# Two more head pairs in cluster order, sorted beside the first batch: routing attention and PReLU feed-forward

## The chip, the cores and the metric

The kernel runs on one core of a Trainium2 chip, as one launch. The metric is the device time of that launch in microseconds (us); less is better. Times given as "the runs" are timed executions without a profiler; the profile is one further execution, recorded by the hardware profiler.

## The reference

Attention with a mask by clusters, then a feed-forward network with PReLU, all in float32 (the weights come as float64):

```
q, k, v: (4 batches, 8 heads, 768 tokens, 64)      centroids: (8 heads, 16, 64)
q_assign = argmax(normalised q . normalised centroids);  k_assign likewise
mask     = q_assign[:, None] == k_assign[None, :]         # same cluster
attn     = softmax(where(mask, q k^T / 8, -1e9));  x = attn v  -> (3072 tokens, 512)
h = x @ w_in (512 x 2048);  g = max(h, 0) + alpha * min(h, 0);  out = g @ w_out (2048 x 512)
```

A query sees only the keys of its own cluster, so most of the 768 x 768 scores of a head are masked away.

## The kernel before, in words

Two heads make a pair; pairs are numbered n = 0 to 15, four to a batch. The work on one pair is cut into steps. An unordered pair has two halves of 384 queries, and each half has three steps; in it all 768 keys meet those queries, key chunk by key chunk of 128: scores on PE (`score`, L784), exponential on ACT (L802, L805), the mask on DVE (L825; pairs 0 to 3 have it added on PE at L793), sums of the exponentials (`add_up` L835 on DVE, or on PE at L932 in steps 0 to 12), weighing of v on PE (`weigh`, L939). Then the row sums are inverted and spread (L907 to L914, or L945 to L955 in the first steps) and `normalise` (L1042) writes the result to a tile xT. A pair in cluster order takes three steps for both halves. Its tokens were sorted by cluster in advance, so that a chunk of keys meets only a window of queries near it (`window`, 224, 320 or 384 columns in place of twice 384), and `weigh_near` (L972) does likewise; the result is then turned to rows (`to_rows`, L1002), scattered back to token order (`put_back`, L1011, indirect DMA from POOL), fetched and transposed (`fetch_back`, `turn_back`, L1030).

The sort of a pair (`order_features`, `order_sims`, `order_counts`, `order_begins`, `order_ranks`, `order_rows`, `order_clusters`) is some 20 DVE operations spread over slots. Then `order_stage` (L661, SP) loads rows of q, k and v, 24 calls of `order_scatter` (L675, POOL) write them to a scratch in DRAM in cluster order, and `order_load` (L681 on, SP) reads them back. Ahead of each group of scatters `pace` puts a small copy on ACT (L651) and one on POOL that waits for it (L652); eight such tokens may be open.

The weights are converted from float64 in 32 tiles (`convert`): SP loads a tile to one of the raw buffers (L247), `split` is two DVE operations (L253, L255), `scale` two on ACT (L259, L261), `join` two on DVE (L265, L268) and a multiply on POOL (L271). Conversions are begun by `convert_next` at fixed slots; `advance` puts scale 4 slots after split and join 2 after that.

Order is written out by hand. A loop over steps u (0 to 23 are batch 0, with the conversion; from 24 on the rest) with five slots to a step emits everything; each engine works in that order. `later(k, piece)` emits a piece k slots on, `prep_at` and `load_at` hold what is due at a step. The FFN of each finished half (`ffn_pieces`: `hidden` L1066 with L1072 and L1058, `final` L1084) is cut into pieces that are fed between the steps' slots: FFN of batch 0, half 0, in steps 12 to 23, then one half at a time. The last batch's FFN (L1246, L1302) comes at the end with nothing beside it. In the kernel before, pairs from NO = 9 on are in cluster order: batch 2 begins with 9, 10 and 11, then 8; batch 3 is 12 to 15.

Of the kernel before, what the change touches and what calls it, by code (L numbers as in the profile page):

```python
# [19 lines left out]
P = 128  # L20
# [3 lines left out]
def kernel(  # L24
# [49 lines left out]
    ps_m = fast.enter_context(tc.tile_pool(name="ps_m", bufs=1, space=PS))  # L74
    ps_f = fast.enter_context(tc.tile_pool(name="ps_f", bufs=2, space=PS))
    fast.enter_context(tc.manual_schedule())
    first_part = fast.enter_context(ExitStack())
    memp = first_part.enter_context(tc.tile_pool(name="memp", bufs=NCH))
    raws = first_part.enter_context(tc.tile_pool(name="raws", bufs=1))
    cvt = first_part.enter_context(tc.tile_pool(name="cvt", bufs=3))  # L80

    early = []

# [18 lines left out]


    pairs = [(b, hp) for b in range(B) for hp in range(NCH)]
    NO = WHOLE * NCH - 3
    NP = len(pairs)
    raw_qk, vts = {}, {}

# [130 lines left out]

    CW = 512  # L240

    raw_tiles = [raws.tile([P, CW, 2], U32, name=f"raw{i}") for i in range(5)]

    def convert(src, dst):
        raw = raw_tiles[0]
# [51 lines left out]
    def advance(stages):  # L297
        stages.pop(0)()
        if stages:
            later(4 if len(stages) == 2 else 2, lambda: stages and advance(stages))  # L300
        elif stages is under_way[0]:
            under_way.popleft()
            converted[0] += 1
# [184 lines left out]
    assert NX * TS == S and 2 * TS == P  # L488
    PARTS = 3
    STAGES = 2  # L490
    us, ranks, orders, scratch, sorts = {}, {}, {}, {}, {}
    sorting = deque()

    def second_part():

        first_part.close()
        for name, bufs in (("emore", 1), ("ordc", 1), ("ordp", 1), ("order", NP - NO),
                           ("xmore", 1), ("byrow", 1), ("pace", 8)):
            sorts[name] = fast.enter_context(tc.tile_pool(name=name, bufs=bufs))
        for i in range(5):  # L500
            e_tiles.insert(0, sorts["emore"].tile([P, 2, HS], FP32, name=f"more{i}"))

    def order_constants():
# [54 lines left out]
                                    scalar2=None, op0=ALU.add)  # L558
        for i, piece in enumerate((columns, sums_before, sums_within, shifts)):
            later(5 + i, piece)  # L560
        begins = ordc.tile([P, NP - NO], FP32, name="begins")
        sorts.update(stage=stage, number=number, place=place, before=before, within=within,
                     shift=shift, begins=begins)

# [40 lines left out]
    def order_ranks(n, ps):  # L605
        member, count = us.pop(n)
        ordp, order = sorts["ordp"], sorts["order"]
        begin = ordp.tile([P, 2], FP32, name="begin")
        nc.vector.tensor_tensor(out=begin, in0=ps[:, 0:2], in1=sorts["shift"], op=ALU.add)
        nc.vector.tensor_copy(out=sorts["begins"][:, n - NO:n - NO + 1], in_=ps[:, 0:1])  # L610
        nc.vector.scalar_tensor_tensor(out=count, in0=count, scalar=begin[:, 1:2],
                                       in1=member, op0=ALU.add, op1=ALU.mult)
        later(1, lambda: order_rows(n, begin, count))
# [113 lines left out]
    assert NJ == GROUP * SB and SB == GT  # L727
    steps, begun_at, feeds = [], [], {}
    for b in range(B):
        whole = [n for n in range(b * NCH, (b + 1) * NCH) if n >= NO]  # L730
        rest = [n for n in range(b * NCH, (b + 1) * NCH) if n < NO]
        begun_at.append(len(steps))
        steps += [(n, None, s) for n in whole for s in range(SB)]
        for half in range(2) if rest else ():
            if half and not whole:
                begun_at.append(len(steps))
            steps += [(n, half, s) for n in rest for s in range(SB)]
            feeds[len(steps)] = [(b, 0), (b, 1)] if whole else [(b, half)]
    begun_at.append(len(steps))
    assert NJ == 6 and GROUP == 2  # L740

# [133 lines left out]
        accTs[n, half] = accT  # L875

    def rows_sums(n, half):
        near = n >= NO
        if not near or half == 0:
            parts[n] = rdp.tile([P, 1 + near, 2, NX], FP32, name="parts" if near else "part")  # L880
        nc.vector.tensor_reduce(
            out=parts[n][:, half if near else 0].rearrange("p h x -> p (h x)"),
            in_=accTs.pop((n, half)), axis=AX.X, op=ALU.add)
# [25 lines left out]
            spread_out(n, half, inv)  # L909

    def spread_out(n, half, inv):
        pool = sorts["ordp"] if n >= NO and half else rdp
        rd = rds[n, half] = pool.tile([P, HS], FP32, name="rd")
        nc.vector.transpose(out=rd, in_=inv[:, :, None].broadcast_to((P, NX, Q)))  # L914

# [117 lines left out]

    def x_tile(b, half):
        if (b, half) not in xTs:
            pool = sorts["xmore"] if (b, half) == (WHOLE - 1, 1) else xpool
            xTs[b, half] = pool.tile([P, NCH, HS], FP32, name="xT")
        return xTs[b, half]

# [102 lines left out]
    def last_pieces():  # L1142
# [195 lines left out]
            return [p1, p5, p6, p2, p7, p3, p4]  # L1338

        def room_for_y():  # L1340
            t = sorts["xmore"].tile([P, NCH, HS], FP32, name="xT").rearrange(
                "p c q -> p (c q)")
# [22 lines left out]
    FREE = SLOTS * SB - 3  # L1365


    ORDERS = [26, 29, 35, 38, 41, 56, 60]
    LEADS = [4, 3, 4, 4, 3, 3, 3]
    prep_at, load_at = {}, {}  # L1370
    for (n, half), u in start_of.items():
        def at(step, slot, piece):
            prep_at.setdefault((step, slot), []).append(piece)
        if half is None:
            t = ORDERS[n - NO]
# [4 lines left out]
            load_at.setdefault(u - LEADS[n - NO], []).append(  # L1380
                lambda n=n: order_load(n))
            at(u - 4, 0, lambda n=n: prep_clusters(n))
            for i in range(2):
                at(u - 1, i, lambda n=n, i=i: order_blocks(n, i))
                at(u - 1, FIRST + i, lambda n=n, i=i: order_queries(n, i))
            continue
        if half == 0:
            if n < NCH:
                if n > 1:
                    load_at.setdefault(max(u - 7, 0), []).append(lambda n=n: load(n))  # L1390
                if n > 0:
                    load_at.setdefault(max(u - 6, 0), []).append(lambda n=n: load_v(n))
            else:
                load_at.setdefault(u - (9 if u < 2 * TOGETHER else 10), []).append(
                    lambda n=n: load(n))
# [8 lines left out]
            at(u - (3 if n < NCH else 5 if u - 6 < TOGETHER else 6), FIRST,  # L1404
               lambda n=n: prep_sims(n)) if u - 6 < 2 * TOGETHER else at(
                   u - 6, FIRST + 1, lambda n=n: prep_sims(n))
# [14 lines left out]
    def scatters_at(v, s, i):  # L1421


        if v < SB:
            return 1 + (s == 0 or i == 0)
        if v < 3 * SB:
            return 0
        if v < 4 * SB:
            return int(s == 0 or i == 0)
        return 1 + (s == 0 or i % 2 == 0)  # L1430

    def feed(pieces):
        for _ in range(pieces):
# [27 lines left out]
    for u in range(-AHEAD, TOGETHER):  # L1461
        for piece in load_at.get(u, []):
            piece()
        n, half, s = steps[max(u, 0)]
        prior = steps[max(u - 1, 0)]
        ended = u > 0 and prior[2] == SB - 1
        tick()
# [26 lines left out]
            whole = len(ffn) - KEEP  # L1494
        take = (max(len(ffn) - KEEP - whole * (UB - 1 - u % UB) // UB, 0) if ffn else 0)

        converting = 0 if u < 0 else (2, 0, 2, 2, 0, 2, 1, 1, 1, 1, 1, 1)[u] if u < UB else 2
        for i in range(SLOTS - FIRST):
            tick()
            feed(take * (i + 1) // 3 - take * i // 3)  # L1500
# [4 lines left out]
                convert_next()  # L1505
            if u >= -1:
                fetch(3 if u < UB else 2)
        if s == SB - 1 and u >= UB:
            total(n)
    assert not sources and not under_way and not unfinished[0]  # L1510
# [5 lines left out]
    for u in range(TOGETHER, NS + 1):  # L1516
# [49 lines left out]
            slots = range(3, SLOTS)  # L1566
        else:
            slots = range(SLOTS)
        if u == TOGETHER + 1:
            order_constants()  # L1570
        for i in slots:
            tick()
            if s == 0:
# [39 lines left out]
    NN, m = NP - NO, 2 * NC  # L1613
# [204 lines left out]
```

## Time and profile before

| | us |
|---|---|
| median of 3 runs | 952.11 |
| the runs | 950.09, 952.11, 956.48 |
| the profiled execution, whole | 932.13 |
| its span | 930.4 |
| PE busy in the span | 916.0 |
| DVE busy | 654.3 |
| POOL busy | 389.1 |
| ACT busy | 262.2 |

The granted clock of TensorE is 1.00 over the whole span. Matmuls overlap in the records, so the busy time of a group of matmuls counts an overlapped stretch once, while the mean of one does not; a matmul of float32 stands as two records. Busy PE is not PE at its peak. The scores of step 6 begin at 46.0 us, those of step 12 at 73.3, those of step 24 at 195.4, those of step 48 (the first pair in cluster order) at 439.2.

### The profile page before, as it was taken

The page shows a single profiled execution, that of the slowest core. Times are in us where ns is not written, and L with a number is a line of the kernel's source. Part 1 is how long each engine was busy: PE and PEld are TensorE (multiplying, and loading weights), DVE is VectorE, ACT ScalarE, POOL GpSimd, SP SyncE. Part 2 cuts the span into 40 slices and gives each one's busy share as a digit, 9 for nine tenths or more (in the row PEclk, how much of TensorE's full clock was granted, in tenths as well). Part 3 has the DMA queues.
Part 4 walks back from the last instruction along what each step waited for, and adds up shares of the span by engine and source line. Part 5 has one row for each costly group of instructions (what it writes and reads, how often), then busy time and mean ns, then how long its engine had stood idle before and what let it go on. Part 6 is the DMA issues. An engine that isn't in the chain of part 4 may idle for free.

```text
span 930.4 us, 11983 instructions
## 1 busy us (share of the span) xinstructions
PE 916.0 (98%) x3963; PEld 494.6 (53%) x3963; DVE 654.3 (70%) x1246; ACT 262.2 (28%) x660; POOL 389.1 (42%) x579
## 2 busy tenths in 40 slices
PE   8999999999999999999999999999999999999997
PEld 5534444445445454455555554555555555556886
DVE  5797788889769699598997899764647135598200
ACT  5764454223123122232222332122222121221000
POOL 2433232200006768587766787677723470000000
PEclk9999999999999999999999999999999999999999
DMA  8433659028001625453762283643511012000000
GB/s 301 132 123 93 148 128 159 18 56 179 26 1 51 153 73 145 88 107 85 156 133 42 50 136 96 142 87 95 97 37 27 12 38 54 1 0 1 23 23 26
DMA packets 226708, 77.71 MB, mean 84 GB/s; under 512 B 210752, under 2 KB 214544, under 8 KB 226640
## 3 DMA queue, kind: packets, MB, share of 16 engines
q1 hardware_dynamic: 217728, 62.72, 30.6%
q0 software_dynamic: 8064, 13.78, 4.7%
q8 instruction: 33, 0.54, 0.3%
q10 hardware_dynamic: 848, 0.39, 0.2%
q14 instruction: 35, 0.29, 0.1%
HBM read 52.25 MB, written 24.25 MB: 82 GB/s over the span
## 4 chain that ended last, share of the span: by engine, by line
PE 94%; DVE 4%; issue 1%; POOL 0%; ACT 0%; DVEq 0%; ACTq 0%; POOLq 0%
PE fps L1066 27%; PE fps L1084 27%; PE sps L784 7%; PE vps L939 7%; PE sps L1302 4%; PE sps L1246 4%; PE fps L784 3%; PE vps L1246 2%; PE vps L1302 2%; PE vps L972 1%; PE mps L972 1%; PE fps L1302 1%; PE fps L1246 1%; PE sps L793 1%; PE mps L894 1%
## 5 line engine op out<-in xcount | busy, mean ns | idle before, releaser
L1066 PE MATMUL fps<-xT,w_in_sb 128*128 128x384 f32 x768 | 259.3, 491 | 0.0
L1084 PE MATMUL fps<-w_out_sb,gT 128*128 128x512 f32 x576 | 254.1, 595 | 0.3 <-DVE gT L1058 0.3
L675 POOL DMA_INDIRECT scratch<-stage,off x168 | 181.3, 1079 | 67.1 <-DMA stage<-in_v_dram 29.5
L1066 PEld LDWEIGHTS fps<-xT,w_in_sb 128*128 128x128 f32 x768 | 142.3, 190 | 103.2 <-issue 4.9
L1084 PEld LDWEIGHTS fps<-w_out_sb,gT 128*128 128x128 f32 x576 | 107.5, 190 | 132.2 <-issue 122.6
L1072 ACT COPY gT<-fps 128x384 f32<-128x384 f32 x96 | 46.0, 479 | 235.9 <-PE fps L1066 235.9
L652 POOL COPY paced<-pace 1x1 f32<-1x1 f32 x204 | 55.0, 270 | 135.7 <-ACT pace L651 135.2
L1058 DVE SCALAR_TENSOR_TENSOR gT<-gT,alpha 128x384 f32<-128x384 f32 x96 | 61.5, 648 | 60.8 <-ACT gT L1072 60.7
L1011 POOL DMA_INDIRECT back<-rows,off x84 | 85.6, 1018 | 22.2 <-issue 16.5
L784 PE MATMUL sps<-qkT 64*128 64x384 f32 (+1 forms) x464 | 85.0, 485 | 0.0
L805 ACT ACTIVATE E<-sps 128x768 f32<-128x768 f32 (+1 forms) x76 | 56.3, 786 | 62.1 <-PE sps L793 39.7
L784 PEld LDWEIGHTS sps<-qkT 64*128 64x128 f32 x464 | 41.2, 186 | 38.6 <-issue 15.5
L825 DVE SCALAR_TENSOR_TENSOR more<-aq,key,more 128x384 f32<-128x384 bf16 (+2 forms) x116 | 60.4, 579 | 0.0
L939 PE MATMUL vps<-E,vt 128*64 128x384 f32 x292 | 54.2, 495 | 1.5 <-DVE xT L1042 1.5
L271 POOL TENSOR_TENSOR w_in_sb<-w_in_sb,power 128x512 f32<-128x512 f32 x16 | 26.9, 1684 | 67.4 <-DVE w_in_sb L268 67.4
L271 POOL TENSOR_TENSOR w_out_sb<-w_out_sb,power 128x512 f32<-128x512 f32 x16 | 22.5, 1411 | 56.0 <-DVE w_out_sb L268 56.0
L825 DVE SCALAR_TENSOR_TENSOR E<-aq,key,E 128x384 f32<-128x384 bf16 (+2 forms) x88 | 45.0, 569 | 0.6 <-ACT E L802 0.6
L835 DVE TENSOR_TENSOR acc<-acc,E 128x768 f32<-128x768 f32 x35 | 33.3, 951 | 14.5 <-ACT E L805 13.6
L907 DVE RECIPROCAL inverses<-mps 64x12 f32<-64x12 f32 (+1 forms) x42 | 10.5, 249 | 45.7 <-PE mps L894 39.8
L1090 ACT COPY y<-fps 128x512 f32<-128x512 f32 x18 | 10.6, 587 | 99.2 <-PE fps L1084 99.2
L1092 DVE TENSOR_TENSOR y<-y,fps 128x512 f32<-128x512 f32 x24 | 16.4, 682 | 27.6 <-PE fps L1084 27.6
L805 ACT ACTIVATE more<-sps 128x768 f32<-128x768 f32 (+1 forms) x40 | 29.2, 764 | 12.2 <-PE sps L784 11.8
(284 smaller groups left out, 1174.1 us busy)
## 6 DMA issues: line engine op xcount, KB each, us to landing
raw<-in_moe_w_in_dram SPq DMA_DIRECT2D x16, 512.0 KB, 5.2
raw<-in_moe_w_out_dram SPq DMA_DIRECT2D x16, 512.0 KB, 4.3
out_dram<-y SPq DMA_DIRECT2D x21, 256.0 KB, 2.4
qk<-scratch SPq DMA_DIRECT2D x56, 96.0 KB, 3.5
qk<-in_q_dram SPq DMA_DIRECT2D x48, 96.0 KB, 3.6
qk<-in_k_dram SPq DMA_DIRECT2D x48, 96.0 KB, 3.6
w_in_kept<-w_in_sb SPq DMA_DIRECT2D x8, 512.0 KB, 3.3
vt<-in_v_dram SPq DMA_DIRECT2D x9, 384.0 KB, 6.5
```

Source lines behind the costliest of these rows:

```text
L652: nc.gpsimd.tensor_copy(out=sorts["paced"], in_=token)
L675: nc.gpsimd.indirect_dma_start(out=scratch[n][1][h * NX + xx], out_offset=bass.IndirectOffsetOnAxis(ap=ranks[n][:, xx, h:h + 1], axis=0), ...
L784: nc.tensor.matmul(out=bank(ps, h, m), lhsT=qkT[r:r + D, S + c * P:S + (c + 1) * P], rhs=qkT[r:r + D, tokens], start=True, stop=not early_ ...
L805: nc.scalar.activation(out=E[:, :, 0:m], in_=ps[:, :, 0:m], func=AF.Exp, scale=SCALE)
L825: nc.vector.scalar_tensor_tensor(out=e, in0=of, scalar=keys[n][:, NJ + c, h:h + 1], in1=e, op0=ALU.is_equal, op1=ALU.mult)
L939: nc.tensor.matmul(out=po[r:r + D, 0:HS], lhsT=vts[n][:, h, c, :], rhs=e[:, h, :], start=(c == 0), stop=(c == NJ - 1))
L1011: nc.gpsimd.indirect_dma_start(out=to[i], out_offset=bass.IndirectOffsetOnAxis(ap=place[:, h, j:j + 1], axis=0), in_=rows[j // HJ][:, j % ...
L1058: nc.vector.scalar_tensor_tensor(out=gs[f], in0=gs[f], scalar=alpha[:, f:f + 1], in1=gs[f], op0=ALU.mult, op1=ALU.max)
L1066: nc.tensor.matmul(out=ps[:, 0:HS], lhsT=w_in_sb[:, c, f * P:(f + 1) * P], rhs=xTs[b, half][:, c, :], start=(c == 0), stop=(c == NCH - 1))
L1084: nc.tensor.matmul(out=ps[:, 0:DM], lhsT=gs[f][:, i * P:(i + 1) * P], rhs=w_out_sb[:, f, :], start=on and f == f0, stop=off and f == f0 + ...
L1246: nc.tensor.matmul(out=bank[to], lhsT=w_in_form(m, x, cc), rhs=rhs[:, cc, :], start=start and cc == 0, stop=cc == KH - 1, skip_group_check ...
L1302: nc.tensor.matmul(out=bank[to], lhsT=g_form(m, x, t), rhs=w_out_form(n, x), start=start and x == 0, stop=x == NQ - 1, skip_group_check=no ...
```

## The change

Pairs 6 and 7, the last two of batch 1, are put in cluster order too. Batch 1 now begins with 6 and 7 (three steps each), then half 0 of pairs 4 and 5, then half 1; it has 18 steps in place of 24. Their sort is done in steps 7 to 23, beside batch 0 and the conversion of the weights, at the slots of the first loop. For the room that the sort's tiles take, the raw buffers go from five to three, the buffers for `power` from three to two, and the conversion's stages follow each other sooner (3 slots and 1 in place of 4 and 2). Sorts of later pairs get other steps (`ORDERS`, `LEADS`), and the scatters per slot are set anew. The core of the diff; renamed pools, index changes of the same kind and the check's wider tables are left out:

```diff
+    sorts = {name: fast.enter_context(tc.tile_pool(name=name, bufs=bufs)) for name, bufs in
+             (("ordc", 1), ("ordp", 1), ("order", 7), ("pace", 8))}
...
-    cvt = first_part.enter_context(tc.tile_pool(name="cvt", bufs=3))
+    cvt = first_part.enter_context(tc.tile_pool(name="cvt", bufs=2))
...
-    NO = WHOLE * NCH - 3
+    ORDERED = [2 * NCH - 2, 2 * NCH - 1] + list(range(WHOLE * NCH - 3, B * NCH))
+    NO = ORDERED[2]
...
-    raw_tiles = [raws.tile([P, CW, 2], U32, name=f"raw{i}") for i in range(5)]
+    raw_tiles = [raws.tile([P, CW, 2], U32, name=f"raw{i}") for i in range(3)]
...
-            later(4 if len(stages) == 2 else 2, lambda: stages and advance(stages))
+            later(3 if len(stages) == 2 else 1, lambda: stages and advance(stages))
...
-        whole = [n for n in range(b * NCH, (b + 1) * NCH) if n >= NO]
-        rest = [n for n in range(b * NCH, (b + 1) * NCH) if n < NO]
+        whole = [n for n in range(b * NCH, (b + 1) * NCH) if n in ORDERED]
+        rest = [n for n in range(b * NCH, (b + 1) * NCH) if n not in ORDERED]
...
-            feeds[len(steps)] = [(b, 0), (b, 1)] if whole else [(b, half)]
+            feeds[len(steps)] = [(b, half)] if b < WHOLE - 1 else [(b, 0), (b, 1)]
...
-        pool = sorts["ordp"] if n >= NO and half else rdp
+        pool = sorts["ordx"] if n in ORDERED and half else rdp
...
-            pool = sorts["xmore"] if (b, half) == (WHOLE - 1, 1) else xpool
+            pool = sorts["xmore"] if (b, half) in ((1, 1), (B - 1, 0)) else xpool
...
-    ORDERS = [26, 29, 35, 38, 41, 56, 60]
-    LEADS = [4, 3, 4, 4, 3, 3, 3]
+    ORDERS = [8, 11, 26, 29, 32, 35, 38, 50, 54]
+    LEADS = [4, 3, 4, 3, 4, 4, 3, 3, 3]
...
-            return 1 + (s == 0 or i == 0)
+            return 1 + (s == 0 or i != 1)
...
-        return 1 + (s == 0 or i % 2 == 0)
+        return 1 + (s == 0 or i != 1)
...
+        if u == ORDERS[0] - 1:
+            order_constants()
...
-        converting = 0 if u < 0 else (2, 0, 2, 2, 0, 2, 1, 1, 1, 1, 1, 1)[u] if u < UB else 2
+        converting = 0 if u < 0 else (2, 0, 2, 1, 1, 1, 2, 1, 1, 1, 1, 1)[u] if u < UB else 2
...
+            if sorting:
+                pace()
+            room = 1 + (i < 2)
+            while sorting and room:
+                scatters, piece = sorting.popleft()
+                piece()
+                room -= scatters
...
-        if u == TOGETHER + 1:
-            order_constants()
```

The last added block stands in the first loop's slots: with sorts pending, each of a step's last three slots takes a pace token and two, two and one scatters.

More of the change, by code (lines that the diff above doesn't have):

```diff
@@ L490 @@
     STAGES = 2
-    us, ranks, orders, scratch, sorts = {}, {}, {}, {}, {}
+    us, ranks, orders, scratch = {}, {}, {}, {}
     sorting = deque()
@@ L496, in second_part @@
         first_part.close()
-        for name, bufs in (("emore", 1), ("ordc", 1), ("ordp", 1), ("order", NP - NO),
-                           ("xmore", 1), ("byrow", 1), ("pace", 8)):
-            sorts[name] = fast.enter_context(tc.tile_pool(name=name, bufs=bufs))
+        for name in ("emore", "ordx", "xmore", "byrow"):
+            sorts[name] = fast.enter_context(tc.tile_pool(name=name, bufs=1))
         for i in range(5):
@@ L560, in order_constants @@
             later(5 + i, piece)
-        begins = ordc.tile([P, NP - NO], FP32, name="begins")
+        begins = ordc.tile([P, len(ORDERED)], FP32, name="begins")
         sorts.update(stage=stage, number=number, place=place, before=before, within=within,
@@ L609, in order_ranks @@
         nc.vector.tensor_tensor(out=begin, in0=ps[:, 0:2], in1=sorts["shift"], op=ALU.add)
-        nc.vector.tensor_copy(out=sorts["begins"][:, n - NO:n - NO + 1], in_=ps[:, 0:1])
+        i = ORDERED.index(n)
+        nc.vector.tensor_copy(out=sorts["begins"][:, i:i + 1], in_=ps[:, 0:1])
         nc.vector.scalar_tensor_tensor(out=count, in0=count, scalar=begin[:, 1:2],
@@ L734 @@
         for half in range(2) if rest else ():
-            if half and not whole:
+            if half and b < WHOLE - 1:
                 begun_at.append(len(steps))
             steps += [(n, half, s) for n in rest for s in range(SB)]
-            feeds[len(steps)] = [(b, 0), (b, 1)] if whole else [(b, half)]
+            feeds[len(steps)] = [(b, half)] if b < WHOLE - 1 else [(b, 0), (b, 1)]
     begun_at.append(len(steps))
@@ L877, in rows_sums @@
     def rows_sums(n, half):
-        near = n >= NO
+        near = n in ORDERED
         if not near or half == 0:
@@ L1340, in room_for_y @@
         def room_for_y():
-            t = sorts["xmore"].tile([P, NCH, HS], FP32, name="xT").rearrange(
+            t = xpool.tile([P, NCH, HS], FP32, name="xT").rearrange(
                 "p c q -> p (c q)")
@@ L1374 @@
         if half is None:
-            t = ORDERS[n - NO]
+            t = ORDERS[ORDERED.index(n)]
             load_at.setdefault(t, []).append(lambda n=n: load(n))
@@ L1379 @@
             at(t + 2, 2, lambda n=n: order_sims(n))
-            load_at.setdefault(u - LEADS[n - NO], []).append(
+            load_at.setdefault(u - LEADS[ORDERED.index(n)], []).append(
                 lambda n=n: order_load(n))
-            at(u - 4, 0, lambda n=n: prep_clusters(n))
+            sooner = u - 1 < TOGETHER
+            at(u - 4, FIRST if u - 4 < TOGETHER else 0, lambda n=n: prep_clusters(n))
             for i in range(2):
-                at(u - 1, i, lambda n=n, i=i: order_blocks(n, i))
-                at(u - 1, FIRST + i, lambda n=n, i=i: order_queries(n, i))
+                at(u - 1, i + FIRST * sooner, lambda n=n, i=i: order_blocks(n, i))
+                at(u - 1, FIRST + i + sooner, lambda n=n, i=i: order_queries(n, i))
             continue
@@ L1393 @@
             else:
-                load_at.setdefault(u - (9 if u < 2 * TOGETHER else 10), []).append(
+                load_at.setdefault(u - (9 if u < start_of[NO, None] else 10), []).append(
                     lambda n=n: load(n))
@@ L1404 @@
             at(u - (3 if n < NCH else 5 if u - 6 < TOGETHER else 6), FIRST,
-               lambda n=n: prep_sims(n)) if u - 6 < 2 * TOGETHER else at(
+               lambda n=n: prep_sims(n)) if u < start_of[NO, None] else at(
                    u - 6, FIRST + 1, lambda n=n: prep_sims(n))
@@ L1611 @@
                             scalar2=good[:, 1:2], op0=ALU.is_le, op1=ALU.mult)
-    NN, m = NP - NO, 2 * NC
+    NN, m = len(ORDERED), 2 * NC
     spans = const.tile([m, 4, NN], FP32, name="spans")
```

## The prediction

> **What bounds the kernel now.** I read the page's busy shares first, then the chain that ended last, then busy time by stretch, then the timelines of PE and DVE around the one place where the chain leaves PE.
>
> ```profile
> PE 916.0 (98%) x3963; PEld 494.6 (53%) x3963; DVE 654.3 (70%) x1246; ACT 262.2 (28%) x660; POOL 389.1 (42%) x579
> PE 94%; DVE 4%; issue 1%; POOL 0%; ACT 0%; DVEq 0%; ACTq 0%; POOLq 0%
> ```
>
> PE carries 94% of the chain, so a matmul saved is time saved, unless another engine is late there. The second line also says where that happens: DVE has 4%. Busy time by stretch (columns: stretch, length, then PE, PEld, DVE, ACT, POOL) shows it is local:
>
> ```profile
> 14.00:34.00 20.00, 19.24 (x188) 9.10 (x186) 13.70 (x32) 15.14 (x24) 4.17 (x2) 1.00 0.56 199
> 46.00:77.00 31.00, 29.54 (x263) 12.08 (x260) 28.42 (x59) 20.86 (x32) 12.90 (x9) 1.00 0.42 133
> 77.00:106.00 29.00, 28.75 (x104) 13.30 (x100) 20.62 (x37) 11.67 (x21) 6.37 (x4) 1.00 0.26 76
> 106.00:146.00 40.00, 40.00 (x155) 18.83 (x154) 33.06 (x60) 17.98 (x30) 11.12 (x8) 1.00 0.77 161
> ```
>
> From 46 to 77 us (steps 6 to 11 and the head of 12: half 0 of batch 0, beside the weights' conversion) DVE is busy 92%, as full as PE. The timelines of PE and DVE at that place:
>
> ```profile
> 67.66 1.51 PE L939 MATMUL vps<-E,vt 128*64 128x384 f32 x8 [1.46 <-DVE xT L1042]
> 59.09 1.50 DVE L255 TENSOR_SCALAR w_in_sb<-raw 128x512 uint32<-128x512 uint32 x1
> 72.54 1.49 DVE L253 TENSOR_SCALAR power<-raw 128x512 uint32<-128x512 uint32 x1 [1.17 <-POOL w_in_sb L271]
> ```
>
> PE stood 1.46 us for a normalisation that DVE reached late. DVE itself waited 1.17 us for a POOL multiply, then ran at a third of its speed. Last, the chain's pieces for one pair's weighing, unordered (one half) and ordered (both halves):
>
> ```profile
> 541.93 4.02 PE vps L939 x24
> ...
> 615.50 1.72 PE vps L972 x16
> 617.21 1.57 PE mps L972 x16
> ```
>
> **What the Trainium skill says.** TensorEngine Tiling (Array Packing), section When to Use Tiling: a contraction of 64 rows can be packed twice. The trace agrees: four score matmuls of 384 columns on 64 rows (8 records) take 1.49 us in the chain, four FFN matmuls on 128 rows (8 records) 2.58. So I price scores and weighing from the chain, not from the 500 ns means. SBUF — State Buffer, section Who interferes with whom: the port pair shared by VectorE and GpSimd is an exclusive lock for a whole instruction. The trace agrees: the split's second operation is 0.42 us mostly and 1.50 when POOL multiplies. TensorE: Matmul & The Clock Gate, section Architectural detail: ACT and DVE are strict FIFO. The 1.46 us above is that: the normalisation stood behind conversions in DVE's queue. Perfetto Trace Analysis, section Optimization Strategy, says that the most-contended engine can change from regime to regime; the stretches show it.
>
> **The change, part by part.**
>
> *Pairs 6 and 7 scored in windows.* Unordered, each half costs scores 4.42 us (two calls of 2.21 on the PE timeline) and weighing 4.02, so a pair 16.9. Ordered: scores 2 x 1.83, weighing 1.72 + 1.57 = 3.29, plus three transposes to rows twice (6 x 0.164 from the group's 6.9 us by 42 = 1.0) and the begin sums (0.35): 8.3. Assignment matmuls are four either way. Two pairs: 2 x 8.6 = 17.2 us off PE, from batch 1 on, where PE is busy all the time. This is the gain.
>
> *Sorting moved into steps 7 to 23.* Constants now go out at step 7, pair 6's sort at steps 8 to 13, pair 7's at 11 to 16. DVE work by the rows (us): constants 0.55 + 0.63 + 0.99 + 0.44 = 2.6; per pair, transposes of q and k 2 x 0.964 = 1.93, the six argmax operations 0.58 + 0.55 + 0.57 + 0.36 + 0.55 + 0.54 = 3.14, member 0.55, scan 0.95, ranks 0.92, offsets 1.35, clusters 1.45.
>
> *First stage, to step 12.* Before pair 3's normalisation at step 12 DVE gains constants, pair 6's transposes, argmax and member: 2.6 + 1.93 + 3.14 + 0.58 = 8.2 us. The conversions from the end of normalisation 0 (34.1) to the end of normalisation 3 (78.96) are as many as before: ten splits, eleven joins. In that stretch DVE idled only 1.16 + 1.17 + 0.53 = 2.9 us. And its queue is less well filled: the join follows its split after 3 + 1 slots in place of 4 + 2, and with one conversion a step there is often nothing between the two on DVE. Then it waits for ACT's 0.72 + 0.62 = 1.34 us. I count this for the splits of steps 4, 5 and 8 in full and for two more in part: 5 us. The scale now also stands on ACT ahead of the exponentials of the very next step (before: of the step after that), and those free the two PSUM score buffers, so DVE's lag reaches PE a step of 4.15 us earlier. The sum is 8.2 + 5 - 2.9 = 10.3. The first FFN matmul (step 12) needs all four chunks of xT, so all DVE lag must be paid there. Least: idle time swallows its 2.9 and no serial waits come, 5.3. Most: contention and POOL's constants standing before its multiplies add 3, so 13. I take 9.5.
>
> *Steps 12 to 23.* DVE gains 11 us in steps 12 to 16 (scan, pair 7's sort) and loses 7 in 17 to 20 (prep of pairs 4 and 5, now at 23 to 28). Step 13 alone asks 14.8 us of DVE against 10.5 of PE. The slopes of step 13 stood at 94.15 us, just before the last matmul that uses them, and DVE had 3.8 us of idle ahead of step 13's sums. With some 3 us more before the sums and 3.4 us of ranks, offsets and simT after them the slopes are about 3.2 late; a second, smaller stop at step 17. POOL gets five scatters a step (1.08 + 0.2 each), three pace copies and two multiplies (2 x 1.55): about 10.4 us against steps of 8.7 to 12.2, and with two power buffers the second split of a step waits for the multiply just issued, about 1 us. The raw tile for that split is loaded after a join of the same step, with 4 to 6 us of DVE work between and 4.3 to 5.2 us to land; SP takes it behind stage loads that wait for scatters. I take 4 us for all; least 2, most 10 if POOL's lag is carried over by every split.
>
> *Batches 1 and 2.* The loads of sorts 6 and 7 (12 DMAs, SP some 6 us each) go out a step or more before use. In steps 30 to 35 put-backs of 6 and 7 meet the scatters of 9 and 10: POOL is asked for 39 + 40 us against 26 + 36 of PE, so it falls about 17 us behind; the eight pace tokens then hold ACT (before, the wait of pace on POOL was 10.7 us in all, without PE stopping). DVE is 7 us behind in the first of these blocks; before, the block at 383 to 408 us was 7 behind and lost 1.7. I take 2, from 0 to 5. Then batch 1's FFN, spread over 6 steps in place of 12, makes blocks of 45 to 52 us of PE in which all catch up. SBUF-only moves (ordx, xmore, memory of the pools) and nine columns in place of seven at the end cost nothing: the last FFN covers them (PE is back to back from 851 us), or some 0.1 us uncovered.
>
> **Sum.** -17.2 + 9.5 + 4 + 2 = -1.7 us on the profiled execution of 932.1 (span 930.4), so 930.4. The runs' median, 952.1, lies 20 above that execution and their spread is 6.4; the difference is carried over: 950.4. About 1% (9.5 us) is what a measurement of this kernel tells from no change.
>
> **Rivals.**
> 1. Forecast: the saving is made on PE and mostly paid back at steps 7 to 17: 950.4, own range 944 to 958. Chance 0.50.
> 2. The front hides it: DVE's idle and the slack at 77 to 106 (20.6 of 29 busy) swallow most. Losses 5.3 + 2 + 0 = 7.3: 952.1 - 9.9 = 942; with the whole gain 935. For: over steps 0 to 23 DVE is not full on average (81% from 77 to 195). Against: the order in the queue, and 92% from 46 to 77. Chance 0.29.
> 3. Slower: POOL becomes the pacer of steps 13 to 20. Each step's multiplies stand behind five scatters, the second split waits for them, and every later DVE operation with it. At 10.4 us of POOL plus some 2 us of waits for stage loads against a mean step of 10.1, each of 8 steps loses 2 us, 16 in place of 4, with 10.3 at the front and 3 in batch 1: -17.2 + 29.3 = +12, 964. It decides once POOL needs over about 11.5 us a step. For: before, scatters waited 29.5 us for stage loads. Against: DVE may lag half a step before PE feels it. Chance 0.21.
>
> **How the numbers follow.** Faster by over 1% needs losses under 7.7 us: rival 2, 0.29. Slower by over 1%: rival 3, 0.21. The range reaches from 938, inside rival 2, to 963, close to rival 3, and leaves about 2 in 10 out.
>
> **What would show it.** Right: a first FFN matmul some 10 us later than 77.4, with PE waits for DVE xT or ACT E between 50 and 90 us; step 24's scores near 209 us in place of 195.4; DVE near 97% from 46 us on; 17 us less PE time from there to the end. Wrong: the first FFN matmul within 5 us of 77.4 (rival 2), or POOL without idle from step 13 to 20 and steps of 12 us (rival 3). If the weighing of pairs 6 and 7 were not 3.3 us each, the gain itself would be wrong.

## The result and the profile after

The changed kernel takes 983.53 us (median of four runs, 980.32 to 985.84), the kernel before 953.26 (950.09 to 956.48) beside it: a ratio of 1.0315, 95% interval 1.0268 to 1.0362. The forecast of 950.4 and its range up to 963 were both wrong; the nearest case was rival 3 (964).

The runs come from several chips, on some of which the kernel before takes 952 to 958 us (the slower kind below) and on others 933 (the faster kind), as in the profile shown of it, so the ratio of every experiment is taken against before on its own chip, and spans are compared across the two kinds only up to step 24, where the two runs of after in the table below differ by 2.4 us.

The page of after, busy shares, granted PE clock in 40 slices, and the chain that ended last:

```profile
PE 925.7 (94%) x3899; PEld 498.1 (51%) x3899; DVE 653.4 (66%) x1244; ACT 258.5 (26%) x674; POOL 468.4 (48%) x689
PEclk9978999989999989999999999899999999999999
PE 72%; DVE 12%; issue 5%; POOL 4%; DMA 3%; SPq 2%; ACT 1%; DVEq 0%; POOLq 0%; ACTq 0%
```

There are 64 matmul records fewer (3,899 against 3,963), as intended, and yet PE is busy 9.7 us longer than in before's profile, and still 2.6 us longer (918.6) in e9, a run of this kernel on a chip of before's kind: it runs part of the time at a lower clock. PE's share of the chain fell from 94% to 72%. Busy time by stretch (stretch, length, then PE, PEld, DVE, ACT, POOL, granted clock, DMA share, GB/s):

```profile
14.00:34.00 20.00, 19.25 (x195) 9.32 (x190) 16.14 (x34) 15.71 (x25) 4.34 (x3) 1.00 0.48 150
50.90:88.50 37.60, 31.90 (x234) 12.27 (x232) 31.35 (x65) 18.17 (x27) 12.29 (x16) 0.81 0.51 116
88.50:136.00 47.50, 42.67 (x185) 19.93 (x183) 41.03 (x76) 19.43 (x40) 22.54 (x26) 1.00 0.49 119
136.00:181.00 45.00, 42.45 (x157) 19.34 (x158) 36.38 (x61) 18.93 (x40) 37.89 (x45) 0.96 0.42 131
195.00:234.50 39.50, 30.44 (x110) 13.63 (x106) 20.14 (x32) 9.46 (x20) 22.56 (x29) 0.91 0.60 110
```

The first 34 us are as before (PE 19.25 of 20). Steps 6 to 11, 27.2 us before (46.04 to 73.25), last 37.7 here (50.89 to 88.56), with DVE at 83% and the clock at 0.81. DVE isn't fuller than before; it waits. From 136 to 181 POOL is busy 37.9 of 45 us (before, 10 of 35 from 146), and from 195 to 234.5 PE stands a quarter of the time. The timelines of PE, ACT and DVE in the first of these places, steps 6 to 11:

```profile
61.91 1.56 PE L787 MATMUL sps<-qkT 64*128 64x384 f32 x8
70.64 2.93 PE L787 MATMUL sps<-qkT 64*128 64x384 f32 x8 [4.51 <-ACT E L808]
...
67.85 0.72 ACT L262 ACTIVATE power<-power,low_exp 128x512 uint32<-128x512 uint32 x1 [3.18 <-DVE power L256]
69.79 0.79 ACT L808 ACTIVATE E<-sps 128x768 f32<-128x768 f32 x1
...
65.72 1.76 DVE L271 SCALAR_TENSOR_TENSOR w_in_sb<-raw,w_in_sb 128x512 f32<-128x512 uint32 x1
67.40 0.41 DVE L256 TENSOR_SCALAR power<-raw 128x512 uint32<-128x512 uint32 x1
```

Read it from the bottom. DVE's split (L256) comes at 67.40. ACT's scale (L262) had stood 3.18 us for it, and the exponentials (L808) behind the scale free the score buffer only then; PE stood 4.51 us. After that wait the same eight score records take 2.93 us in place of 1.56. The waits of ACT over the whole run, of before and of after (us in total, times, longest):

```profile
ACT power L259 <- DVE power L253: 3.2, 2, 2.2
ACT pace L651 <- POOL paced L652: 10.7, 5, 3.0
```

```profile
ACT power L262 <- DVE power L256: 57.9, 18, 9.1
ACT pace L654 <- POOL paced L655: 24.8, 16, 3.3
```

The second place is what is emitted at step 20. PE meets it in step 21, which takes 21.1 us (193.87 to 215.01) in place of 9.5. The timelines of SP, DVE and PE there:

```profile
194.59 1.19 SPq L691 DMA_DIRECT2D off<-scratch  x2
195.88 5.00 SPq L700 DMA_DIRECT2D qk<-scratch  x8
200.98 1.50 SPq L709 DMA_DIRECT2D vt<-scratch  x2
202.58 0.56 SPq L250 DMA_DIRECT2D raw<-in_moe_w_out_dram  x1
...
207.66 0.43 DVE L256 TENSOR_SCALAR power<-raw 128x512 uint32<-128x512 uint32 x1 [8.11 <-DMA raw<-in_moe_w_out_dram]
...
209.62 5.46 PE L1069 MATMUL fps<-xT,w_in_sb 128*128 128x384 f32 x8 [6.31 <-DVE y L1095]
```

The last raw load of the weights stands behind the twelve loads of pair 6's sorted rows in SP's queue, and DVE, with everything behind that split, stands 8.11 us; PE then stands 6.31 for DVE's y, and its next eight records take 5.46. The third place is the block of step 33. The timelines of ACT, DVE and PE:

```profile
350.86 0.19 ACT L654 COPY pace<-ones 1x1 f32<-1x1 f32 x1 [2.83 <-POOL paced L655]
354.75 0.19 ACT L654 COPY pace<-ones 1x1 f32<-1x1 f32 x1 [2.39 <-POOL paced L655]
354.84 0.46 ACT L1075 COPY gT<-fps 128x384 f32<-128x384 f32 x1
...
355.34 0.62 DVE L1061 SCALAR_TENSOR_TENSOR gT<-gT,alpha 128x384 f32<-128x384 f32 x1 [5.98 <-ACT gT L1075]
355.94 0.15 DVE L613 COPY begins<-mps 128x1 f32<-128x1 f32 x1
...
356.20 1.73 PE L577 MATMUL mps<-qk,cT 128*32 128x384 f32 x8 [3.73 <-issue]
```

ACT's copy of gT stood behind pace tokens that POOL had not yet taken; DVE's gT behind ACT; the begins, which free the one PSUM buffer that L577 needs, behind DVE's gT. The wait is booked as "issue", but its end is the begins' end.

The saving itself is there. The timeline of pair 6's weighing, both halves, 3.35 us from first start to last end:

```profile
263.50 1.79 PE L975 MATMUL vps<-more,vt 128*64 128x384 f32 x16
...
266.14 0.71 PE L975 MATMUL mps<-more,vt 128*64 128x96 f32 x8
```

The starts of the scores of some steps, read off PE's timeline of each kernel (us), place the loss. The first column of "after" is the profile shown, from a chip of the slower kind; the second (e9 below) is a run on a chip of the kind on which before takes 933, as in its profile. From step 24 on only the second can be set against before: what the slower kind does there is said at e5.

| | before | after | after (e9) |
|---|---|---|---|
| step 12 | 73.25 | 88.56 | 85.94 |
| step 13 | 85.34 | 102.33 | 100.03 |
| step 24 | 195.37 | 234.55 | 232.14 |
| end of span | 930.4 | 984.1 | 969.4 |
| to step 13 | 85.3 | +17.0 | +14.7 |
| step 13 to 24 | 110.0 | +22.2 | +22.1 |
| step 24 to the end | 735.0 | +14.6 | +2.3 |

### The profile page after: what moved, and what is told of

The parts are those of the page before. It is cut to its first block, busy times and chain, and to the rows that moved or that the text cites. A ratio compares the mean times of both kernels' runs of the same rounds, so it can differ in the third digit from the quotient of the medians.

```text
span 984.1 us, 12151 instructions
## 1 busy us (share of the span) xinstructions
PE 925.7 (94%) x3899; PEld 498.1 (51%) x3899; DVE 653.4 (66%) x1244; ACT 258.5 (26%) x674; POOL 468.4 (48%) x689
## 4 chain that ended last, share of the span: by engine, by line
PE 72%; DVE 12%; issue 5%; POOL 4%; DMA 3%; SPq 2%; ACT 1%; DVEq 0%; POOLq 0%; ACTq 0%
PE fps L1069 21%; PE fps L1087 20%; PE sps L1305 4%; PE sps L1249 4%; PE sps L787 4%; PE vps L942 3%; POOL scratch L678 2%; PE vps L1249 2%; PE vps L1305 2%; PE fps L787 2%; PE vps L975 1%; PE mps L975 1%; PE fps L1305 1%; PE fps L1249 1%; DVE acc L838 1%
## 5 line engine op out<-in xcount | busy, mean ns | idle before, releaser
L678 POOL DMA_INDIRECT scratch<-stage,off x216 | 227.9, 1055 | 97.8 <-DMA stage<-in_v_dram 42.0
L1087 PE MATMUL fps<-w_out_sb,gT 128*128 128x512 f32 x576 | 258.8, 603 | 7.5 <-DVE gT L1061 3.9
L655 POOL COPY paced<-pace 1x1 f32<-1x1 f32 x230 | 66.1, 287 | 139.1 <-ACT pace L654 130.1
L1014 POOL DMA_INDIRECT back<-rows,off x108 | 111.5, 1033 | 24.0 <-issue 20.6
L1061 DVE SCALAR_TENSOR_TENSOR gT<-gT,alpha 128x384 f32<-128x384 f32 x96 | 57.9, 612 | 76.8 <-ACT gT L1075 61.9
L787 PEld LDWEIGHTS sps<-qkT 64*128 64x128 f32 x432 | 39.6, 193 | 41.8 <-issue 16.6
L808 ACT ACTIVATE E<-sps 128x768 f32<-128x768 f32 (+1 forms) x73 | 53.1, 773 | 15.2 <-PE sps L796 9.0
L828 DVE SCALAR_TENSOR_TENSOR more<-aq,key,more 128x384 f32<-128x384 bf16 (+2 forms) x100 | 50.8, 563 | 1.1 <-issue 0.5
L654 ACT COPY pace<-ones 1x1 f32<-1x1 f32 x230 | 34.9, 185 | 40.1 <-POOL paced L655 24.8
L274 POOL TENSOR_TENSOR w_in_sb<-w_in_sb,power 128x512 f32<-128x512 f32 x16 | 21.4, 1342 | 42.3 <-DVE w_in_sb L271 42.2
L828 DVE SCALAR_TENSOR_TENSOR E<-aq,key,E 128x384 f32<-128x384 bf16 (+2 forms) x80 | 39.8, 555 | 0.0
L262 ACT ACTIVATE power<-power,low_exp 128x512 uint32<-128x512 uint32 x32 | 23.1, 722 | 58.2 <-DVE power L256 57.9
L1093 ACT COPY y<-fps 128x512 f32<-128x512 f32 x18 | 10.6, 586 | 97.4 <-PE fps L1087 88.1
```

The lines of the kernel that those rows point to most:

```text
L655: nc.gpsimd.tensor_copy(out=sorts["paced"], in_=token)
L678: nc.gpsimd.indirect_dma_start(out=scratch[n][1][h * NX + xx], out_offset=bass.IndirectOffsetOnAxis(ap=ranks[n][:, xx, h:h + 1], axis=0), ...
L787: nc.tensor.matmul(out=bank(ps, h, m), lhsT=qkT[r:r + D, S + c * P:S + (c + 1) * P], rhs=qkT[r:r + D, tokens], start=True, stop=not early_ ...
L808: nc.scalar.activation(out=E[:, :, 0:m], in_=ps[:, :, 0:m], func=AF.Exp, scale=SCALE)
L828: nc.vector.scalar_tensor_tensor(out=e, in0=of, scalar=keys[n][:, NJ + c, h:h + 1], in1=e, op0=ALU.is_equal, op1=ALU.mult)
L1014: nc.gpsimd.indirect_dma_start(out=to[i], out_offset=bass.IndirectOffsetOnAxis(ap=place[:, h, j:j + 1], axis=0), in_=rows[j // HJ][:, j % ...
```

## The experiments

In the edits below "..." marks what is cut. Theories: A, the buffers and slots of the conversion make DVE and ACT wait for each other; B, the sorting work on DVE does it; C, the raw load behind the sorted loads; D, POOL's lag in steps 30 to 36.

**e1, the buffers alone.** The kernel before, with these edits, in short form:

```diff
-cvt bufs=3, 5 raw tiles, later(4 ... 2), converting (2, 0, 2, 2, 0, 2, 1, ...)
+cvt bufs=2, 3 raw tiles, later(3 ... 1), converting (2, 0, 2, 1, 1, 1, 2, 1, ...)
```

> The kernel before with the change's buffers and its table of conversions alone: three raw tiles, two power tiles, a join 3 + 1 slots after its split, one conversion a step in steps 3 to 5. No pair is ordered more than before, so nothing is saved and no sorting is moved. Theory A (the buffers make DVE, ACT and DVE wait for each other): the waits of ACT for DVE's power, 3 us before and 58 after, come back, over 20 us of them; the first FFN matmul is 5 us or more later than before's 77.4; the kernel is 6 to 14 us slower than before. Theory B (the sorting work on DVE does it): no more than 2 us slower, first FFN matmul within 2 us of 77.4.

Measured: 965.19 against 955.37, ratio 1.0108 (1.0062 to 1.0153). The first FFN matmul came at 89.20, step 13 at 97.14, 11.8 later than before; from step 13 to 24 111.3 us against 110.0. The wait of ACT:

```profile
ACT power L259 <- DVE power L253: 32.2, 9, 8.2
```

Theory A holds for the first stage, with no sorting there at all. B alone is out.

**e2, one pair ordered, sorted later.** After, with these edits, in short form:

```diff
-ORDERED = [2 * NCH - 2, 2 * NCH - 1] + ...;  ORDERS = [8, 11, 26, ...];  LEADS = [4, 3, ...]
+ORDERED = [2 * NCH - 1] + ...;               ORDERS = [11, 26, ...];     LEADS = [3, ...]
```

> The changed kernel with pair 7 alone ordered in batch 1 (pair 6 as before), its sort begun at step 11, its sorted loads at step 21, behind the last raw load; of the sorting only the constants stay in the first stage. Saving: one pair, 8.6 us by the prediction. Theory A: the buffers' loss stays whole, the first FFN matmul comes 6 to 10 us later than before's 77.4, and the kernel is 0 to 8 us slower than before. Theory B: with the sorting out of the first stage, the first FFN matmul is back within 3 us of 77.4 and the kernel 5 to 9 us faster than before.

Measured: ratio 1.0283 (1.0246 to 1.0321), far slower than either theory gave. Step 12 came at 80.92, 7.7 late, as A has it. Step 24 came at 216.25, 20.9 late though half the sorting was gone. Most of what was lost after step 13 lies in step 18, 20.4 us in place of 12.2: DVE waited there 2.6 us for a POOL multiply and 2.0 for a raw load that stood behind stage loads in SP's queue, PE 4.5 for DVE, and the granted clock was 0.83. That isn't A's (e1 lost 1.3 from step 13 to 24), nor B's, since DVE stood. From step 24 to the end the kernel took 764.9 us; e1 and e14, whose code there is before's, took 751.1 and 758.9 on chips of this kind, so 6 to 14 us of that are this kernel's own. What they are isn't shown.

**e3, the sorted loads behind the raw load.** After, with

```diff
-LEADS = [4, 3, 4, 3, 4, 4, 3, 3, 3]
+LEADS = [3, 3, 4, 3, 4, 4, 3, 3, 3]
```

> The changed kernel with the sorted loads of pair 6 issued at step 21 in place of step 20, so that they stand behind the last raw load of the weights in SP's queue. Theory C (that raw load, 8 us late behind 12 sorted loads, stops DVE and then PE in steps 20 to 22): step 24's scores 9 to 13 us earlier than after's 234.5, the DVE wait of 8.1 us for raw gone, the kernel 9 to 13 us faster than after. Rival (DVE is late in these steps anyway, or the sorted loads now come late for step 23): under 4 us.

Measured: step 24 at 224.40, 10.1 earlier, as theory C says. The time hardly moved: ratio 1.0272 (1.0206 to 1.0338), which overlaps after's. The block of step 36 (from its scores to those of step 39; blocks are three steps long) took 60.1 us in place of 51.8 and that of step 48 28.7 in place of 22.8. So C is right about the place and this run couldn't say what it is worth; e11 does.

**e4, put-backs without tokens.** After, with

```diff
 def put_back(to, place, rows, i):
-    pace()
```

> The changed kernel with no pace token taken by the put-backs of ordered pairs (in all batches); the scatters keep theirs. Theory D (POOL falls behind in steps 30 to 35 and the tokens then hold ACT, whose copies free the FFN's PSUM buffers): the block of step 33, 45.8 us in after, is 6 to 10 us shorter, the kernel 6 to 11 us faster than after. Rival (POOL's work itself, scatters and put-backs, comes too late for what needs it): within 3 us of after, and the wait only changes its name.

Measured: ratio 1.0477 (1.0416 to 1.0539), slower than after. The block of step 33 took 55.7 us, not 36 to 40. Both sides were wrong. e7 and e13 come back to this; why it got slower stays open.

**e5, the kernel before once more.**

> The kernel before, unchanged, for one more profiled execution. The one shown lies 20 us under the median of the timed ones (932 against 953) at a mean granted clock of 1.00, where the timed ones have 0.988 to 0.994. Theory E (the profile shown is an unusually good execution; the usual one has PE gaps late, each followed by some us of a lower clock): 948 to 960 us, step 24's scores near 195 as before, and the missing 15 to 20 us between 470 and 720 us, where the kernel with the buffers alone lost 16 us against the profile shown. Rival (the loss is spread over the whole span, for instance by a slower clock everywhere): step 24 later than 200 us.

Measured: 933.55 us at a clock of 0.999, with seven further runs of before on that chip between 931.87 and 934.42, and step 24 at 195.96. Theory E is wrong as put: the profile shown is like every run on this chip, so it isn't an unusual execution but most likely one from a chip of this kind. The 16 to 24 us by which the slower kind differs do lie late, though. From step 24 to the end before takes 735.0 us in its profile and 735.8 here, and e6 736.5 on this chip, with PE waiting 3 to 4 us in all; on the slower kind e1 and e14, with the same code there, take 751.1 and 758.9, with PE waiting 15.8 and 17.4.

**e6, three raw tiles alone.** The kernel before with `range(5)` made `range(3)`.

> The kernel before with three raw tiles in place of five, and nothing else of the change: three power tiles, joins 4 + 2 slots after their splits and the old table stay. Theory A1 (the tightened power tiles and slots make the loss, not the raw tiles): within 3 us of before, first FFN matmul within 2 us of 77.4. Theory A2 (with three raw tiles the loads come too late for DVE): 6 us or more slower than before, with DVE waiting for raw loads.

Measured: 952.46 against 933.10, ratio 1.0221 (1.0195 to 1.0246). Step 12 at 73.70, untouched; the loss starts at step 17 and is 17.6 us at step 24 (213.53 less before's 195.96 on that chip). The waits of DVE from 74 to 215 us:

```profile
DVE power L253 <- DMA raw<-in_moe_w_out_dram: 15.4, 7, 6.3
DVE power L253 <- DMA raw<-in_moe_w_in_dram: 13.5, 5, 4.7
```

A2, then, but in another stage: with joins 6 slots after their splits, three raw tiles can't feed two conversions a step. The shorter slots of the change give the tiles back earlier, and with them that loss is all but gone (e1: 1.3 us lost from 13 to 24); they pay for it in the first stage.

**e7, no token from step 24 on.** After, with

```diff
 def put_back(to, place, rows, i):
-    pace()
...
-            if room and sorting:
-                pace()
```

> The changed kernel without any pace token from step 24 on (put-backs and scatters); the tokens up to step 23 stay. Theory D1 (the tokens alone tie PE to a POOL that is behind; what POOL owes is not needed yet): the blocks of steps 30 and 33, 30.5 and 45.8 us in after, fall to about 26 and 36, and the kernel is 10 to 16 us faster than after. Theory D2 (POOL's work itself is late: scatters and put-backs are needed by later loads, or without tokens they run in the way of others): same or slower than after, and the waits name scatters, put-backs or their DMAs.

Measured: 961.22, ratio 1.0306 (1.0288 to 1.0323); after on a chip of that kind (e9) has 969.81, so 8.6 us gained, a little under the 10 to 16. Block 33, in e9 and in e7, both on chips of the faster kind (stretch, length, PE, PEld, DVE, ACT, POOL, clock, DMA, GB/s):

```profile
329.30:373.00 43.70, 38.85 (x129) 17.76 (x128) 27.93 (x51) 9.64 (x33) 37.58 (x58) 0.96 0.43 104
```

```profile
327.30:363.30 36.00, 36.00 (x127) 16.68 (x126) 28.01 (x51) 5.99 (x11) 28.18 (x31) 1.00 0.41 107
```

PE is back to back, though the put-backs are still POOL's. Block 30 stayed at 30.6: its waits (begins, simT, rows, 4.4 us in all) aren't the tokens'.

**e8, put-backs of pairs 6 and 7 not on POOL.** After, with a plain DMA of SP's queue in their place, which leaves out the way back to token order:

```diff
+        if len(sorts["straight"]) < 4 * NJ:
+            sorts["straight"].append(i)
+            nc.sync.dma_start(out=to[i][h * S + j * P:h * S + (j + 1) * P, :], in_=rows[...])
+            return
```

> The changed kernel with the put-backs of pairs 6 and 7 written straight by SP's queue, with no indirect DMA on POOL and no token for them; their tokens stay in cluster order, so that part of the computation, the way back to token order, is left out for these two pairs. POOL has 24 x 1.6 us = 38 us less to do in steps 28 to 36. Theory D (POOL, asked for more than PE in steps 30 to 36, sets the pace there, whether through tokens or through its own work): the blocks of steps 30, 33 and 36 are 10 to 15 us shorter together than after's 128.1, and the kernel 8 to 15 us faster. Rival (DVE or the SP queue sets it): under 4 us.

Measured: 962.24, ratio 1.0307 (1.0285 to 1.0329), 7.6 us faster than e9. Blocks 30, 33 and 36 take 119.9 together, e9's 128.3. Its block 33:

```profile
330.20:366.20 36.00, 36.00 (x129) 16.67 (x128) 29.75 (x55) 7.32 (x23) 27.15 (x40) 1.00 0.65 158
```

Less work for POOL, with the tokens left on the scatters, gives the same 36.0 as no tokens. Together with e7 and with ACT's waits for tokens in this block (29.3 us in e9, 5.9 here), it says that POOL's lag is the cause and the token the way it reaches PE; the lag alone is not tested, since this edit takes the tokens of these put-backs away too. Theory D holds on this kind of chip, at 8 us and not the 10 to 15 put for these blocks.

**e9, after again.**

> The changed kernel, unchanged, beside before on one chip: the runs so far came from two chips, on which before takes 955 and 933 us, so after needs a time on the chip of the next three. If the loss is the kernel's own (PE gaps to step 24 of 39 us, steps 30 to 36 of 15, less the saving of 17): 34 to 40 us slower than before where before takes 933, 28 to 34 where it takes 955. If the loss were the slower chip's: under 25 where before takes 933.

Measured: 969.81 against 933.06, ratio 1.0388 (1.0371 to 1.0405): 36.7 us, as the first case expected. The loss is the kernel's own.

**e10, the slots.** After, with

```diff
-            later(3 if len(stages) == 2 else 1, ...)
+            later((4 if long else 3) if len(stages) == 2 else (2 if long else 1), ...)
```

where `long` is set in steps that convert one tile.

> The changed kernel with the scale 4 slots after its split and the join 2 after that, as before the change, in the steps that convert one tile (3 to 5, 7 to 11); 3 + 1 stays where two are converted. Buffers as after. Theory A3 (the shorter slots make ACT wait for DVE ahead of the exponentials, and DVE for ACT; the three raw tiles do nothing in this stage): step 12's scores, 88.6 us in after, come 8 to 12 us earlier, and the kernel is 6 to 12 us faster than after on the same chip. Rival A2 (two power and three raw tiles hold the stage whatever the slots): under 3 us.

Measured: 964.14, ratio 1.0345 (1.0328 to 1.0362), 5.7 us faster than e9. Step 12 at 81.43: 4.5 earlier than e9, 7.1 than the profile of after. (Executions with the same code up to there differ by 5 us, as the account below says.) Too much for the rival, less than A3 expected; 8.2 us of lateness stay.

**e11, e3's and e7's edits together.**

> The changed kernel with the sorted loads of pair 6 at step 21, behind the last raw load, and no pace token from step 24 on. Theory C + D1 (both losses are real and add up, now that POOL's lag can't hold ACT): step 24 10 us earlier than after's, the blocks of steps 33 to 39 8 us shorter, so 16 to 20 us faster than after on the same chip. Rival (an earlier start is paid back by a later wait, as with the moved loads alone, which gained 10 us at step 24 and nothing at the end): 6 to 10 us faster.

Measured: 953.20, ratio 1.0224 (1.0207 to 1.0242), 16.6 us faster than e9 and 8.0 faster than e7. Here the moved loads keep what they gain: steps 13 to 24 take 123.1 us in place of e9's 132.1.

**e12, all three edits.**

> The changed kernel with the three edits together: slots 4 + 2 where one tile is converted, the sorted loads of pair 6 behind the last raw load, no pace token from step 24 on. If the losses add up: 24 to 30 us faster than after on the same chip, within 12 us of before. Rival (they share one limit, DVE's queue up to step 23): 14 to 20 us faster than after.

Measured: 946.44, ratio 1.0141 (1.0124 to 1.0158), 23.4 us faster than e9; the parts, 5.7 and 16.6, make 22.3, so the losses add up. It is still 13.4 slower than before, against the 12 expected.

**e13, no scatters for pairs 6 and 7.** e12, with eight plain loads a pair in place of stage loads and scatters, and with no tokens for them, so that these two pairs aren't in cluster order:

```diff
+        if n < 2 * NCH:
+            ... nc.sync.dma_start(out=whole[r0:r0 + S, d0:d0 + D], in_=src[b, 2 * hp + h]) ...
+            return
```

> The kernel with the three edits (e12), but the tokens of pairs 6 and 7 go to the scratch memory straight from q, k and v by eight loads of SP's queue for each pair, in token order: their scatters on POOL, the stage loads and the pace tokens for them are left out, and so these two pairs are scored in an order that isn't the clusters' (the ranks are still worked out on DVE). Theory P (POOL's 5 scatters a step hold the multiplies, and these the two power tiles and so DVE's splits): steps 13 to 24, 125 us in e12 and 110 in before, fall to 110 to 115, and the kernel is 10 to 15 us faster than e12. Theory V (DVE's own added work, scan, ranks, offsets, features, does it): 120 us or more, and 0 to 5 us faster.

The stretch from step 13 to step 24, of e12 and of e13:

```profile
95.20:220.40 125.20, 113.17 (x433) 50.43 (x433) 99.14 (x161) 48.71 (x106) 91.05 (x107) 0.99 0.49 129
```

```profile
93.80:208.90 115.10, 110.22 (x435) 50.28 (x434) 99.64 (x161) 46.04 (x77) 26.05 (x18) 1.00 0.52 113
```

With the same 161 DVE operations and 65 us less on POOL the stretch is 10.1 us shorter, at the edge of what P expected and three quarters of the 13.6 between e12 and the 111.6 of e14; the other 3.5 may be V's and are not shown to be. But the edit takes away stage loads and tokens as well as scatters: DVE's waits in the stretch fell from 8.4 us for POOL's multiplies and 6.2 for raw loads (e12) to none and 1.8. So the scatters and what goes with them cost the 10 us, in part through POOL and in part through SP's queue. The kernel as a whole was far slower, ratio 1.0782 (1.0725 to 1.0839), on a chip of the other kind, and that comes later. Its timelines of PE, ACT and POOL in the block of step 33:

```profile
340.03 2.29 PE L1085 MATMUL fps<-xT,w_in_sb 128*128 128x384 f32 x3 [25.05 <-issue]
...
339.49 0.49 ACT L822 ACTIVATE more<-fps 128x384 f32<-128x384 f32 x1 [29.95 <-remote]
...
324.05 0.96 POOL L1030 DMA_INDIRECT back<-rows,off  x1 [0.30 <-issue]
325.32 0.96 POOL L1030 DMA_INDIRECT back<-rows,off  x1 [0.31 <-issue]
326.59 0.96 POOL L1030 DMA_INDIRECT back<-rows,off  x1 [0.30 <-issue]
```

PE and ACT stand for 25 and 30 us, DVE for 18.8, for nothing the profile names, while POOL issues indirect DMAs every 1.27 us. e4 and e15, also without tokens on put-backs and on chips of the slower kind, lost time after step 24 too (e4 in the same block); e7, e11 and e12, on the other kind of chip, gained. What holds the engines there isn't settled.

**e14, the buffers with slots 4 + 2.** e1 with e10's edit.

> The kernel before with the change's buffers and table of conversions, and the slots 4 + 2 where one tile is converted, 3 + 1 where two are: e1 with the slots of before in steps 3 to 5 and 7 to 11, no sorting added. It parts e10's step 12 (8 us late) into buffers and sorting. Theory S (the slots make the buffers' loss in the first stage; what e10 keeps is sorting work): step 12's scores within 3 us of before's 73.3, where e1 had 85.1, and the kernel within 6 us of before on the same chip. Theory A2 (few buffers lose time whatever the slots): step 12 over 78, 8 us or more slower.

Measured (ten runs): ratio 1.0047 (1.0016 to 1.0077), 4.9 us. Step 12 at 74.47, 1.2 later than before, where e1 was 11.8 later; step 24 at 198.14. Theory S: nearly all of the buffers' loss in the first stage was the slots'. What e10 still had at step 12, 81.43 less 74.47, is put down to the sorting: 7.0 us, from one execution of each, on chips of different kinds.

**e15, one pair, with the edits.** e2 with the edits of e10 and e7.

> Pair 7 alone ordered in batch 1, its sort begun at step 11 (e2), with the edits: slots 4 + 2 where one tile is converted, its sorted loads behind the last raw load, no pace token from step 24 on. The saving is 8.6 us in place of 17.2, against half of the scatters and no sorting but the constants before step 12. If the losses are those named: step 24 at 205 to 210 us, and 0 to 8 us slower than before on the same chip. It beats before only if step 24 comes before 204.

Measured: 1003.86 and 1011.47 in the two fastest of four runs, about 5% over before's 958.06; step 24 at 214.41. Both expectations missed: step 24 was only 1.8 us earlier than in e2, with step 18 at 21.5 us (DVE waited there 3.7 for a POOL multiply and 2.5 for a raw load), and without tokens it lost after step 24 as e13 did. No version beat before.

## Why the prediction was wrong

**The gain was right.** Pair 6's weighing takes 3.35 us where 3.29 was put. From step 24 to the end, at a granted clock of 1.00 in both, PE is busy 726.5 us in before and 709.9 in e7: 16.6 less, where 17.2 was put.

**First stage: 13 against 9.5.** Seven kernels have after's code up to step 12 (after, e3, e4, e7, e8, e9, e11). They begin its scores at 83.33 to 88.58 us, on average 86.6, before and e5 at 73.25 and 73.83. So 13 us were lost, and executions of one code differ by 5. With the old slots (e10 and e12: 81.43 and 82.80) 8.6 were lost, of which e14 has 0.9 from the buffers. That leaves 7.6 for DVE's added work, put at 8.2, and 4.5 for the slots, put at 5. As far as so few executions tell, the step that failed is "- 2.9": DVE's idle time, which was to swallow part of the added work, swallowed next to none. Another sign of that: DVE was to be near 97% busy and was 83%, because it stood too. ACT waited for the split, PE for ACT, and DVE for what those two then delivered late. Alone the slots cost 10.6 (e1's 85.06 less e14's 74.47), so these losses don't simply add.

**Steps 12 to 23: 22 against 4.** Three terms. "The loads of sorts 6 and 7 (12 DMAs, SP some 6 us each) go out a step or more before use" looked at those loads and missed what is queued behind them: one raw load, 9.0 us (e9's 132.1 less e11's 123.1). The working says "SP takes it behind stage loads", but never put the twelve sorted loads and the raw load of the same step side by side. Second, the scatters: "about 1 us" a step for the multiply was priced into rival 3 at 16 for eight steps and into the forecast at part of 4; e13 measures 10.1 for them with their stage loads and tokens. Third, 3.5 us are left that no run ascribes; DVE's lag of 3.2 may be in them.

**Batches 1 and 2: 19.5 against 2** (the 2.3 us of the table and the saving of 17.2 that should have stood there). The lag of 17 us and its way (tokens, ACT) were foreseen, and then a resemblance with a block that lost 1.7 was taken for the price. In e9 block 33 lost 7.7 (43.7 against e7's 36.0; ACT waited 29.3 us for tokens there), block 30 4.4 and block 57 3.4 (48.0 against before's 44.6); the other 4 are spread. "In which all catch up" did not happen for PE: time that the bounding engine has lost stays lost.

**The clock was in no sum.** The Trainium skill, TensorE: Matmul & The Clock Gate, Part 1, section What's actually happening, says that PE falls to half its clock after an idle window of about 3.4 us, that this window is free-running, and that it needs about as long of work to return. These traces agree in the main: after a wait of 4.51 us (after) the score call took 2.93 in place of 1.56, and one and the same wait of 3.40 us, ending at 48 to 49 us, was followed by sixteen small matmuls in 1.98, 1.26 or 1.09 us in three executions (after, e9, e7). But a shorter wait isn't safe: in e12 PE stood 1.81 us before 45.62, and from 46.65 to 49.50 the granted clock was 0.51. e9's mean clock is 0.981, before's 1.00 on such a chip: 0.019 of 969.4, an estimate of about 18 of the 56 us of loss (39.0 of span and the saving of 17.2). PE's own sums agree: its waits came to 44.4 us in e9 and 9.1 in before, 35 more, and it was busy 2.6 longer with 16.6 us less to do, 19 more.

**The base did no harm.** The 20 us between profile and median belong to the chip, and the runs of after came from a chip of the slower kind too. And slower got only 0.21 because rival 3 was drawn with one loss large and the others near the forecast's; measured, all three were large at once. That its 964 came nearest is no merit of its mechanism: POOL's scatters cost 10 us of its 16, and the rest came from terms it had left small.

## What to carry to other kernels

Where PE bounds at 98%, price any wait that the change can give it at its length plus some microseconds at half speed. For a transfer that moves earlier, list not only whether it arrives in time but what stands behind it in its queue. A buffer count, the slots between producer and consumer and the issue order are one setting: three raw tiles for five cost 18 us with the old slots (e6) and, with two power tiles for three, 12 with the new ones (e1), in another stage each, and 3 by step 24 with the slots chosen by step (e14). And before a single profile is split into terms of a few us, look at how far executions of the same code differ: here 5 us by step 12.

## What was not expected of the hardware

One and the same kernel takes 933 us on some chips and 952 to 958 on others, with mean clocks of 0.999 and 0.991, and what a change brings differs with it: after was 3.88% slower on the faster kind and 3.15% on the slower. Each chip was used for one set of runs, so a chip and its hour can't be told apart. On the slower kind, three kernels whose put-backs took no pace tokens (e4, e13, e15) needed 767.6, 816.6 and 795.2 us from step 24 to the end where after needed 749.6, and in one of them PE, DVE and ACT stood together for 19 to 30 us beside POOL's back-to-back indirect DMAs. On the faster kind three such kernels (e7, e11, e12) needed 725.7 to 726.9 where after needed 737.3. That the tokens keep POOL from this on the slower kind is only a guess.
